# Attention with two gated layers on one core: all four full key tiles enter the values' product as float32, and three kinds of tiles span two PSUM banks

## The chip, the core and the metric

One core of a Trainium2 chip runs the whole program. Its engines run from queues of their own: TensorE (PE, with the weight loads shown as PEld), VectorE (DVE), ScalarE (ACT), GpSimd (POOL), and SyncE (SP), which issues all DMAs. The metric is the device time in microseconds, the median of three runs.

## What is computed

```python
# q, k, v: (4, 8, 576, 64) float32
q_rot, k_rot = rotate(q), rotate(k)                    # rotary embedding over d = 64
scores = matmul(q_rot, k_rot.T) / sqrt(64)
attn = exp(scores - max(scores)); attn /= attn.sum() + 1e-9
x = (attn @ v) -> (2304, 512)                          # heads side by side
x = (sigmoid(x @ w_gate) * (x @ w_val)) @ w_out        # d_ff 1536
h = x @ w_in2
out = where(h > 0, h, exp(min(h, 0)) - 1) @ w_out2     # d_ff 2048
```

The weights of the two layers come as float64, q, k and v as float32.

## The kernel before

**Two stages.** The first some 360 us are attention, 32 heads one after the other (in 16 pairs). The two layers follow; they are not touched by the change. In `first_chunk` and `split_all` (L611 to L622, L145) the weights of the first layer's first chunk are taken apart by VectorE, ScalarE and GpSimd while the last heads are still computed.

**Precision.** A product of two float32 matrices is mostly made of three products of `float32r` parts (a high part and the rest). For the scores the parts of q and k stand one above the other in the 128 rows of a buffer `W`, so that two products (`K1` by `Q1`, `K2` by `Q2`) give the sum, and a row of `W` holds the negative maxima, which so come off in the product itself. For the values there are two ways. A *split* tile (`KINDS` names the engine that makes its low part: key tiles 0 and 2 VectorE, tile 1 GpSimd) has its exponential written twice by ScalarE, once as float32 (`e`, L462) and once as float32r (`ph`, L464); `low_part` (L468) subtracts, and three products follow (L497 to L499) with a v that was split by `split_v` (L388). The *full* tile (`KINDS` None: tile 3) is written once and multiplied as float32 (L494). The last 64 keys (t = ST = 4, the tail) are one stack `pt` of high and low part and take two products (L491, L492). Heads 30 and 31 (`LF`) multiply all their tiles as float32 with `last_v` (L487).

**The order of work.** It is written out by hand: a *slot* for each head, of ten *steps* (NSTEP), two for each of the five key tiles. Slot i does the scores of head i, the maxima of head i + 2 and the values of head i - 1, interleaved step by step (L623 to L637); `at(slot, step, f)` puts anything else beside a step (with .5 ahead of the next step's scores, else behind its values). Every engine takes its instructions in the order in which they are written. A step of slot i is: two score products of one half (288 columns) of key tile t (L459), ScalarE's exponentials, one maxima product (L409) with VectorE's reduction (L412), and the values of one key tile for one half (L482 on). The scores and the transposes of q and k (`split`, L316) take one-bank tiles from `ps_qk` (3 buffers), the maxima from `ps_mt` (3), the values from `ps_pv` (2).

**Maxima.** `max_row` (L420) transposes a head's maxima, ScalarE copies the row, and a DMA puts it into `W`, where that head's scores need it. It is at step 1.5 of the slot ahead of the head, `max_all` (which joins the two halves' maxima) at step 2, so for all but head 0 the row holds the first half's maxima alone.

**SP's queue** carries, in the order of the text: loads of k and q (L599, step 0 of even slots), tails (L602), v (L603: three loads of 256-byte pieces for a group of four heads, at slot 4g - 1, step 6, and `load_vf` for the full tile), the moves of q's and k's parts into `W` (`move`, L344), the row of maxima (L426), and the four short transfers of the sums' reciprocals (`inverse`, L519).

**GpSimd** does the rotary embedding of all pairs but the first (`rope_ops`, L286), the low part of tile 1, v's low parts and the normalization (L545).

## Time and profile before

| | us |
|---|---|
| median of 3 runs | 1217.23 (1215.57 to 1217.28) |
| the profiled execution's own time | 1214.78 |
| its span, first to last instruction | 1213.0 |
| attention up to the first product of the layers | 364.73 |
| from there to the end | 848.27 |

| busy of the span | PE | PEld | DVE | ACT | POOL |
|---|---|---|---|---|---|
| us | 1163.2 | 983.2 | 995.6 | 499.4 | 689.2 |

The trace gives start and duration of every instruction, and for idle time the event that ended it. A matmul's record is longer than its share of TensorE: records overlap, and the pace is the distance from start to start in a stretch without waits. A float32 matmul is recorded as two (x2).

### The profile page before, as it was taken

The page shows a single profiled execution, that of the slowest core. Times are in us where ns is not written, and L with a number is a line of the kernel's source. Part 1 is how long each engine was busy: PE and PEld are TensorE (multiplying, and loading weights), DVE is VectorE, ACT ScalarE, POOL GpSimd, SP SyncE. Part 2 cuts the span into 40 slices and gives each one's busy share as a digit, 9 for nine tenths or more (in the row PEclk, how much of TensorE's full clock was granted, in tenths as well). Part 3 has the DMA queues.
Part 4 walks back from the last instruction along what each step waited for, and adds up shares of the span by engine and source line. Part 5 has one row for each costly group of instructions (what it writes and reads, how often), then busy time and mean ns, then how long its engine had stood idle before and what let it go on. Part 6 is the DMA issues. An engine that isn't in the chain of part 4 may idle for free.

```text
span 1213.0 us, 17583 instructions
## 1 busy us (share of the span) xinstructions
PE 1163.2 (96%) x5956; PEld 983.2 (81%) x5956; DVE 995.6 (82%) x2024; ACT 499.4 (41%) x1251; POOL 689.2 (57%) x731
## 2 busy tenths in 40 slices
PE   5898999999889999999999999999999999999998
PEld 4787888887857888888888888888888887888887
DVE  8888887887798987867777676778999999999844
ACT  3777777877744532122222222344422222222221
POOL 8977888887355555443444344666554545545421
PEclk9999999999999999999999999999999999999999
DMA  7676666755523121111111111101111111110004
GB/s 186 138 154 140 137 151 140 158 131 128 137 73 97 36 70 53 51 37 36 53 39 49 52 36 35 35 20 51 53 35 53 35 52 36 53 36 18 1 35 122
DMA packets 71146, 89.53 MB, mean 74 GB/s; under 512 B 35920, under 2 KB 44400, under 8 KB 71056
## 3 DMA queue, kind: packets, MB, share of 16 engines
q1 hardware_dynamic: 71056, 88.41, 28.4%
q8 instruction: 47, 0.77, 0.3%
q14 instruction: 43, 0.35, 0.1%
HBM read 56.01 MB, written 4.87 MB: 50 GB/s over the span
## 4 chain that ended last, share of the span: by engine, by line
PE 58%; DVE 9%; ACT 1%; issue 0%
PE h L680 12%; PE h L681 12%; PE h L682 12%; PE o L680 8%; PE o L681 8%; PE o L682 8%; DVE z L763 2%; DVE g L706 1%; DVE g L705 1%; DVE ca L130 1%; DVE cm L137 1%; DVE cm L127 1%; DVE ce L124 1%; DVE ce L133 1%; DVE cm L125 1%
## 5 line engine op out<-in xcount | busy, mean ns | idle before, releaser
L712 POOL TENSOR_TENSOR gl<-g,gh 128x512 fp32r<-128x512 f32 (+1 forms) x140 | 168.6, 1204 | 326.2 <-ACT gh L711 260.4
L711 ACT CAST gh<-g 128x512 fp32r<-128x512 f32 (+1 forms) x140 | 81.2, 580 | 306.6 <-DVE g L706 172.0
L459 PE MATMUL s<-W 128*128 128x288 f32 (+1 forms) x640 | 164.2, 339 | 22.9 <-DMA W<-row 9.6
L680 PE MATMUL h<-xh,wh 128*128 128x512 f32 (+1 forms) x480 | 177.3, 369 | 1.7 <-ACT xh L665 1.3
L681 PE MATMUL h<-xl,wh 128*128 128x512 f32 (+1 forms) x480 | 177.5, 370 | 1.0 <-DVE xl L666 1.0
L682 PE MATMUL h<-xh,wl 128*128 128x512 f32 (+1 forms) x480 | 177.1, 369 | 0.0
L138 POOL TENSOR_TENSOR ca<-ca,wh 128x256 f32<-128x256 f32 x136 | 113.8, 837 | 94.6 <-DVE cm L134 89.0
L412 DVE TENSOR_REDUCE MX<-mt 128x1 f32<-128x288 f32 (+1 forms) x320 | 132.6, 444 | 23.4 <-PE mt L409 22.0
L462 ACT ACTIVATE e<-s 128x288 f32<-128x288 f32 (+1 forms) x320 | 127.7, 411 | 50.1 <-PE s L459 10.8
L135 ACT CAST wh<-ca 128x256 fp32r<-128x256 f32 x136 | 55.3, 407 | 215.9 <-DVE ca L130 215.9
L459 PEld LDWEIGHTS s<-W 128*128 128x128 f32 (+1 forms) x640 | 101.1, 185 | 48.2 <-ACT ph L464 13.8
L140 POOL TENSOR_TENSOR wl<-ca,cm 128x256 fp32r<-128x256 f32 x136 | 113.0, 831 | 18.5 <-DVE cm L137 11.4
L681 PE MATMUL h<-yl,wh 128*128 128x512 f32 (+1 forms) x320 | 117.7, 368 | 0.0
L682 PE MATMUL h<-yh,wl 128*128 128x512 f32 (+1 forms) x320 | 117.7, 368 | 0.0
L680 PE MATMUL h<-yh,wh 128*128 128x512 f32 (+1 forms) x320 | 117.7, 368 | 0.0
L680 PE MATMUL o<-wh,gh 128*128 128x512 f32 x288 | 112.8, 392 | 1.6 <-DVE z L763 1.2
L681 PE MATMUL o<-wl,gh 128*128 128x512 f32 x288 | 112.2, 390 | 0.0
L682 PE MATMUL o<-wh,gl 128*128 128x512 f32 x288 | 112.1, 389 | 0.0
L701 DVE TENSOR_TENSOR g<-h,g 128x512 f32<-128x512 f32 (+1 forms) x60 | 38.2, 637 | 88.6 <-PE h L682 85.8
L409 PE MATMUL mt<-W 128*128 128x288 f32 (+1 forms) x320 | 100.5, 322 | 7.5 <-DVE MX L412 4.5
L680 PEld LDWEIGHTS h<-xh,wh 128*128 128x128 f32 x480 | 90.9, 189 | 17.9 <-ACT xh L665 1.7
L681 PEld LDWEIGHTS h<-xl,wh 128*128 128x128 f32 x480 | 90.8, 189 | 16.4 <-DVE xl L666 1.5
(116 smaller groups left out, 2875.2 us busy)
## 6 DMA issues: line engine op xcount, KB each, us to landing
W<-hl SPq DMA_DIRECT2D x89, 288.0 KB
raw<-in_moe_w_out_dram SPq DMA_DIRECT2D x28, 512.0 KB
raw<-in_moe_w_in_dram SPq DMA_DIRECT2D x16, 512.0 KB
raw<-in_moe_w_gate_dram SPq DMA_DIRECT2D x12, 512.0 KB
raw<-in_moe_w_val_dram SPq DMA_DIRECT2D x12, 512.0 KB
rb<-d SPq DMA_DIRECT2D x32, 144.0 KB
k<-in_k_dram SPq DMA_DIRECT2D x16, 256.0 KB
q<-in_q_dram SPq DMA_DIRECT2D x16, 256.0 KB
```

What stands on the lines that cost most here:

```text
L135: nc.scalar.copy(h, a)
L138: nc.gpsimd.tensor_tensor(out=a, in0=a, in1=h.bitcast(F32), op=ALU.subtract)
L140: nc.gpsimd.tensor_tensor(out=l, in0=a, in1=mf, op=ALU.add)
L409: nc.tensor.matmul(m[0:n, 0:HS], lhsT=operand(i, "Q1", t * P, n), rhs=operand(i, "K1", a * HS, HS), start=True, stop=True)
L412: nc.vector.tensor_reduce(out=MX[i % 3][0:n, a, t : t + 1], in_=m[0:n, 0:HS], axis=AX.X, op=ALU.max, negate=True)
L459: nc.tensor.matmul(s, lhsT=operand(i, st, t * P, n), rhs=operand(i, mv, a * HS, HS), start=st == "K1", stop=st == "K2")
L462: nc.scalar.activation(e[:, c], s, AF.Exp)
L680: nc.tensor.matmul(ps, lhsT=ah, rhs=bh, start=j == 0, stop=False)
L681: nc.tensor.matmul(ps, lhsT=ah, rhs=bl, start=False, stop=False)
L682: nc.tensor.matmul(ps, lhsT=al, rhs=bh, start=False, stop=j == n - 1)
L711: nc.scalar.copy(hi, g)
L712: nc.gpsimd.tensor_tensor(out=lo, in0=g, in1=hi.bitcast(F32), op=ALU.subtract)
```

## The change

All four full key tiles are handled as the full tile was, in all 32 heads; `KINDS`, `LF`, `last_v` and the split of v's full tiles go. Scores, maxima and the transposes of q or k use tiles of two banks, one half (288 columns) in each, and one exponential, one reduction (over both axes) or one copy handles both; so `max_all` goes. `ps_qk` has 2 such tiles, `ps_mt` 1. v of four heads comes in one load and GpSimd copies it into `VF`. The two half-wide products of the rotary embedding become one with the halves' order reversed in the read. Steps move: `max_row` from 1.5 to 0.5, k's and q's loads from step 0 to 3 (tails 4), v's load from slot 4g - 1 step 6 to slot 4g - 2 step 8, `split_v` from steps 1 and 5 to 5 and 7, a pair's transposes from four places (5.5 to 10.5) to two (5.5 and 9.5), the first move from step 11 to 12.

```diff
-    KINDS = ("vector","gpsimd","vector",None)
-        ps_qk = ...tile_pool(name="ps_qk", bufs=3, ...)
-        ps_mt = ...tile_pool(name="ps_mt", bufs=3, ...)
+        ps_qk = ...tile_pool(name="ps_qk", bufs=2, ...)
+        ps_mt = ...tile_pool(name="ps_mt", bufs=1, ...)
 def load_v(g):
-            t = raws["v", g] = v_p.tile([P, 4, NS, D], F32, tag="v", name=f"v{g}")
-            for n in range(NS):
-                nc.sync.dma_start(out=t[:, :, n], in_=tiles_of_v(b, h, 4, SP[n]))
+            load("v", 4 * g, 4, v_p)
             load_tails("vv", g, v_p)
-        def load_vf(pr): ...
 def rope_ops(pr, which, eng):
-            for a in range(2):
-                lo, hi = slice(a * hd, (a + 1) * hd), slice((1 - a) * hd, (2 - a) * hd)
-                tt(out=sv[..., lo], in0=x[..., hi], in1=sin[..., lo], op=ALU.mult)
-                yield
+            two = lambda y: y.rearrange(f"{axes} (two d) -> {axes} two d", two=2)
+            tt(out=two(sv), in0=two(x)[..., ::-1, :], in1=two(sin), op=ALU.mult)
+            yield
 def split(pr, which):          # one tile for all five transposes
+            T = ps_qk.tile([P, 1024], F32, tag="qk", name=f"T{which}{pr}")[:, 0:S]
...
             nc.scalar.copy(hi, T)
             nc.vector.tensor_tensor(out=lo, in0=T, in1=hi.bitcast(F32), op=ALU.subtract)
 def split_v(pr, piece):
             if piece == 0:
-                nc.scalar.copy(vs[..., D : 2 * D], x)
-                nc.gpsimd.tensor_tensor(out=vs[..., 0:D], in0=x, in1=vs[..., D : 2 * D].bitcast(F32), op=ALU.subtract)
+                nc.gpsimd.tensor_copy(VF[par][..., 0:D], x)
+        def both_halves(ps, n):
+            return ps.rearrange("p (a s) -> p a s", a=2)[0:n, :, 0:HS]
 def maxima(i, h):              # at odd steps, both halves
+            m = both_halves(ps_mt.tile([P, 1024], F32, tag="mt", name=f"mt{i}_{t}"), n)
+            for a in range(2):
+                nc.tensor.matmul(m[:, a], lhsT=operand(i, "Q1", t * P, n), rhs=operand(i, "K1", a * HS, HS), ...)
+            nc.vector.tensor_reduce(out=MX[i % 3][0:n, t : t + 1], in_=m, axis=AX.XY, op=ALU.max, negate=True)
-        def max_all(i): ...
 def max_row(i):
-            m = ps_mt.tile([P, 512], F32, tag="mt", name=f"mr{i}")
+            m = ps_qk.tile([P, 1024], F32, tag="qk", name=f"mr{i}")
 def scores(i, h):              # at even steps, both halves
+                e = probs[i, t] = e_p.tile([P, S], F32, tag="ef", name=f"e{i}_{t}", bufs=2 * ST)
+            s = both_halves(ps_qk.tile([P, 1024], F32, tag="qk", name=f"s{i}_{t}"), n)
+            for st, mv in (("K1", "Q1"), ("K2", "Q2")):
+                for a in range(2):
+                    nc.tensor.matmul(s[:, a], lhsT=operand(i, st, t * P, n), rhs=operand(i, mv, a * HS, HS), ...)
+            nc.scalar.activation(e.rearrange("p (a s) -> p a s", a=2), s, AF.Exp)
+            if t == ST:
+                nc.scalar.activation(probs[i, t][TL:P]..., s, AF.Exp)
+                at(i, h + 2.5, low_part, e, probs[i, t])
 def values(i, h):
+            if t == ST:  ...            # the two products of the tail, as before
+            else:
+                nc.tensor.matmul(out_ps, lhsT=VF[par][:, ab, t], rhs=e, start=t == 0, stop=False)
-            at(*((i - 2, 9) if i == 0 else (i - 1, 2)), max_all, i)
-            at(*((i - 2, 9) if i == 0 else (i - 1, 1.5)), max_row, i)
+            at(*((i - 2, 9) if i == 0 else (i - 1, 0.5)), max_row, i)
-                at(s0, (1, 5)[piece], split_v, pr, piece)
+                at(s0, (5, 7)[piece], split_v, pr, piece)
-            slot, step = {3: (-1, 9), 4: (1, 0)}.get(pr, (2 * pr - 8, 0))
+            slot, step = {3: (-1, 9), 4: (1, 3)}.get(pr, (2 * pr - 8, 3))
-            at(4 * g - 1, 6, load_v, g)
+            at(4 * g - 2, 8, load_v, g)
```

## Rows read from the trace of the kernel before

**Rows 1.** Busy time by stretch: window, length, busy us (count) each engine, PEclk, DMA.
```profile
33.28:326.64 293.36, 271.32 (x1734) 238.67 (x1735) 240.81 (x517) 225.63 (x672) 232.78 (x238) 0.97 0.64 143
326.64:364.73 38.09, 31.44 (x166) 24.38 (x164) 36.70 (x84) 21.15 (x62) 21.12 (x24) 0.96 0.26 70
364.73:1213.00 848.27, 840.80 (x3984) 705.95 (x3984) 690.26 (x1364) 240.08 (x488) 406.40 (x422) 1.00 0.15 46
120.40:123.60 3.20, 3.20 (x16) 3.06 (x15) 2.93 (x6) 1.86 (x6) 3.07 (x5) 0.50 0.58 123
349.10:356.30 7.20, 7.14 (x36) 5.20 (x34) 6.93 (x16) 3.90 (x12) 4.36 (x6) 1.00 0.28 75
```

**Rows 2.** TensorE in order of time, slot 29: start, us, line, out<-in, count.
```profile
326.64 0.42 PE L459 MATMUL s<-W 128*128 128x288 f32 x2
...
327.44 0.42 PE L459 MATMUL s<-W 128*128 128x288 f32 x2
...
329.40 0.29 PE L409 MATMUL mt<-W 128*128 128x288 f32 x1
329.53 0.65 PE L494 MATMUL pv<-e,VF 128*128 128x288 f32 x2
...
330.27 0.29 PE L409 MATMUL mt<-W 128*128 128x288 f32 x1
...
330.94 0.29 PE L409 MATMUL mt<-W 128*128 128x288 f32 x1
```

**Rows 3.** TensorE in order of time: slot 31, values in float32; a pair's transposes.
```profile
349.86 0.64 PE L459 MATMUL s<-W 128*128 128x288 f32 x2
350.34 0.65 PE L487 MATMUL pv<-e,last_v 128*128 128x288 f32 x2
350.61 0.64 PE L459 MATMUL s<-W 128*128 128x288 f32 x2
...
301.70 0.38 PE L330 MATMUL Tk<-ident,rk 128*128 128x128 f32 x2
...
302.22 0.47 PE L459 MATMUL s<-W 128*64 128x288 f32 x2
```

**Rows 4.** Waits from 33.28 to 326.64: who waited for whom, us, times, longest.
```profile
PE s L459 <- DMA W<-row: 9.6, 5, 2.2
PE s L459 <- ACT ph L464: 5.5, 5, 3.3
ACT VS L393 <- DMA v<-in_v_dram: 10.8, 7, 4.7
PEld s L459 <- ACT ph L464: 13.6, 29, 3.5
```

**Rows 5.** SP's issues in slot 12, then TensorE at the start of slot 13.
```profile
154.19 1.27 SPq L192 DMA_DIRECT2D k<-in_k_dram  x1
...
157.47 0.76 SPq L426 DMA_DIRECT2D W<-row  x1
...
160.09 0.40 PE L459 MATMUL s<-W 128*128 128x288 f32 x1 [1.83 <-DMA W<-row]
```

**Rows 6.** Groups by shape, 33.28 to 326.64: count, busy us, mean ns, idle before.
```profile
L412 DVE TENSOR_REDUCE MX<-mt 128x1 f32<-128x288 f32 x224 | 94.0, 444 | 20.3 <-PE mt L409 19.1
L464 ACT ACTIVATE ph<-s 128x288 fp32r<-128x288 f32 x168 | 68.2, 406 | 0.0
L471 DVE TENSOR_TENSOR pl<-e,ph 128x576 fp32r<-128x576 f32 x56 | 57.2, 1021 | 0.0
L471 POOL TENSOR_TENSOR pl<-e,ph 128x576 fp32r<-128x576 f32 x28 | 40.1, 1432 | 6.9 <-ACT ph L464 6.9
L471 DVE TENSOR_TENSOR pt<-e,pt 64x576 fp32r<-64x576 f32 x28 | 26.3, 938 | 0.6
```

**Rows 7.** Before the first head's scores: DVE's first maxima, TensorE's first scores.
```profile
14.51 3.85 DVE L412 TENSOR_REDUCE MX<-mt 128x1 f32<-128x288 f32 x10
...
24.96 1.17 PE L459 MATMUL s<-W 128*128 128x288 f32 x4
```

More of the change, by code (lines that the diff above doesn't have):

```diff
@@ L55, in attention_moe_moe_kernel @@
     NC2 = w_in2.shape[1] // FC
-    KINDS = ("vector","gpsimd","vector",None)
-    FP = [t for t, kind in enumerate(KINDS) if kind is None]
-    SP = [t for t, kind in enumerate(KINDS) if kind is not None]
-    NS, NF = len(SP), len(FP)
     assert D == 64 and TL == 64 and NK == NHP
@@ L247, in attention_moe_moe_kernel @@
         W = [[const.tile([P, 4 * S + TL], F32R, name=f"W{par}{ab}") for ab in range(2)] for par in range(NPAR)]
[L250 to L251 removed]
+        VF = [const.tile([P, 2, ST, 2 * D], F32, name=f"VF{par}") for par in range(2)]
         VT = [const.tile([P, 2, 3 * D], F32R, name=f"VT{par}") for par in range(2)]
[L253 removed]
+        MX = [small_p.tile([P, ST + 1], F32, name=f"MX{j}") for j in range(3)]
         def constants(par):
@@ L286, in rope_ops @@
         def rope_ops(pr, which, eng):
-            hd = D // 2
             if which == "t":
@@ L314, in attention_moe_moe_kernel, with split @@
         parts = {}
[L316 to L323 removed]
+        def split(pr, which):
+            if which == "k":
+                parts[pr] = hl_p.tile([P, 4, S], F32R, tag="hl", name=f"hl{pr}")
             r, rt = rot[pr, which], rot[pr, "t"]
             o = 0 if which == "q" else TL
[L326 to L340 removed]
+            T = ps_qk.tile([P, 1024], F32, tag="qk", name=f"T{which}{pr}")[:, 0:S]
+            for c in range(0, SM, P):
+                nc.tensor.transpose(T[:, c : c + P], r[:, c // P].rearrange("p h d -> p (h d)"), ident)
+            nc.tensor.transpose(
+                T[:, SM:S], rt[o : o + TL].rearrange("p h d -> p (h d)"), ident[o : o + TL, o : o + TL]
+            )
+            hi, lo = (parts[pr][:, n] for n in ((0, 1) if which == "k" else (2, 3)))
             nc.scalar.copy(hi, T)
@@ L348, in move @@
             slots = W[pr % NPAR][ab][:, 0 : 4 * S].bitcast(F32).rearrange("p (j s) -> p j s", j=4)
-            if pr == 1:
-                hk, lk, hq, lq = (x.bitcast(F32) for x in parts[pr])
-                nc.sync.dma_start(out=slots[z, 1], in_=lk[r])
-                nc.sync.dma_start(out=slots[r, 0:2], in_=hk[r].unsqueeze(1).to_broadcast([D, 2, S]))
-                nc.sync.dma_start(out=slots[z, 2], in_=hq[r])
-                nc.sync.dma_start(out=slots[r, 2], in_=hq[r])
-                nc.sync.dma_start(out=slots[r, 3], in_=lq[r])
-                return
             src = parts[pr].bitcast(F32)
@@ L455, in scores @@
-            e, hi, lo, _ = probs[i, t]
-            c = slice(a * HS, (a + 1) * HS)
-            s = ps_qk.tile([P, 512], F32, tag="qk", name=f"s{i}_{h}")[0:n, 0:HS]
-            for st, mv in (("K1", "Q1"), ("K2", "Q2")):
-                nc.tensor.matmul(
-                    s, lhsT=operand(i, st, t * P, n), rhs=operand(i, mv, a * HS, HS), start=st == "K1", stop=st == "K2"
-                )
-            nc.scalar.activation(e[:, c], s, AF.Exp)
-            if hi is not None:
-                nc.scalar.activation(hi[:, c], s, AF.Exp)
-                if a == 1:
-                    at(i, h + 1.5, low_part, i, t)
@@ L468, in low_part @@
-        def low_part(i, t):
-            e, hi, lo, _ = probs[i, t]
-            eng = nc.gpsimd if t < ST and KINDS[t] == "gpsimd" else nc.vector
-            eng.tensor_tensor(out=lo, in0=e, in1=hi.bitcast(F32), op=ALU.subtract)
+            if a == 1:
+                return
+            if t == ST:
+                e = e_p.tile([P, S], F32, tag="e", name=f"e{i}_{t}")[TL:P]
+                probs[i, t] = p_p.tile([P, S], F32R, tag="pt", name=f"pt{i}")
+            else:
+                e = probs[i, t] = e_p.tile([P, S], F32, tag="ef", name=f"e{i}_{t}", bufs=2 * ST)
@@ L473, in attention_moe_moe_kernel, with low_part @@
+        def low_part(e, pt):
+            nc.vector.tensor_tensor(out=pt[0:TL], in0=e, in1=pt[TL:P].bitcast(F32), op=ALU.subtract)
         us, sums, ps = {}, {}, {}
@@ L567, in attention_moe_moe_kernel @@
         for which in "kq":
-            for half in range(2):
-                at(-5, 1, split, 0, which, half)
+            at(-5, 1, split, 0, which)
             at(-5, 1, copies, 0, which)
         at(-5, 1, move, 0, 1)
-        for (which, half), st in zip((("k", 0), ("k", 1), ("q", 0), ("q", 1)), (10, 11, 13, 14)):
-            at(-2, st, split, 1, which, half)
+        for which, st in (("k", 11.5), ("q", 13.5)):
+            at(-2, st, split, 1, which)
         at(-1, 10, move, 1, 0)
```

126 lines of the change are left out of this document (24 added, 102 removed).

## The prediction

> **What bounds the kernel now.** I read the busy time by stretch first [rows 1]. From 364.73 on, the layers keep TensorE at 840.80 of 848.27 us; nothing of the change lies there. What it can move is the 365 us ahead: slots 1 to 28 (33.28 to 326.64, 293.4 us or 10.48 a slot), a start of 33.3 us and an end of 38.1 us. Second comes TensorE in order of time. In a stretch without waits a step with a split tile takes 0.80 us (326.64 to 327.44), one with the full tile 0.87 (329.40 to 330.27), a tail step 0.67 (330.27 to 330.94) [rows 2]. The tail step is five float32r products, so one is 0.134. A slot has six, two and two of these: 4.80 + 1.74 + 1.34 = 7.9 us. A pair's q and k add four groups of transposes; one with the tail's takes 0.52 [rows 3], two of the four lack it, so I put 0.4 each: 14 pairs x 4 x 0.4 = 22. Dense, slots 1 to 28 would be 28 x 7.9 + 22 = 243 us. They take 293, so TensorE loses 50 us to waiting although its records show it 271 us busy [rows 1]: records overlap and hide short waits.
>
> Third, the waits. Five heads' scores wait 9.6 us for the row of maxima [rows 4]. In slot 12 its DMA is issued at 157.47, behind k's load of 154.19 and what follows it, and TensorE starts again only at 160.09 [rows 5]. After such a wait the granted clock is 0.50, the 1.2 GHz level: 120.40 to 123.60 is one of five stretches in these slots [rows 1]. At half the clock 3.2 us do the work of 1.6, so they cost about 8 us. ScalarE waits 10.8 us for v's loads, and every exponential queued behind that copy waits too; TensorE's scores wait 5.5 us for ScalarE and its weight loads 13.6, in 29 pieces [rows 4]. The rest of the 50 us is of that short kind: a one-bank tile is released only after two exponentials, and these wait in turn for buffers that the subtractions hold.
>
> **The change, part by part.** *TensorE, slots 1 to 28.* Six split steps a slot become full ones: 0.87 - 0.80 = 0.07 each. From heads 30 and 31, whose values are all float32: a step of 0.75 us (349.86 to 350.61) less two scores at 0.134 is 0.48 for one product [rows 3], against three at 0.134 = 0.40, so 0.08. I take 0.077: 28 x 6 x 0.077 = 13 us more, all on the path. Dense becomes 256.
>
> The Trainium skill, "FP8 and Floating Point Precision" (TensorE Precision Notes), says that true FP32 takes four passes through the array, which speaks against the change. Four passes at the trace's 0.134 would be 0.54 and not 0.48; the trace nearly agrees, and by the rule the slots would lose some 10 us more.
>
> *ScalarE* loses six `ph` exponentials of 0.406 a slot [rows 6] and v's wide copy; wide exponentials save the fixed part of half their number. *VectorE* loses two subtractions of 1.021 a slot, *GpSimd* one of 1.432 [rows 6]; GpSimd gains a copy of v (512 elements a row, no row like it; between nothing and those 1.432, hidden either way, since its next user is five steps off). Ten reductions of 0.444 become five over 576 columns. Bounds for one: two at the pace of the first head's ten, 2 x 3.85/10 = 0.77 [rows 7], or two whole, 0.89 [rows 6]; I take 0.77. The reversed read in the rotary embedding lies between half and the whole of the two products that it replaces, on GpSimd, off the path. None of this lies on the path by itself; it removes what makes the scores wait. I do not price these waits one by one: what counts is what still waits afterwards.
>
> *SP.* The row comes at step 0.5, ahead of all loads (step 3 or 4) and of the first move; it then has some eight steps, over 7 us, where the late one needed about 2.5 (157.47 to 160.09 [rows 5]). The 9.6 us and the low clock behind them go. The load of v is one transfer 8 steps earlier, and its reader is four steps later. But at step 8 it waits in SP's queue for GpSimd's copy of step 5 and the tail's of step 7, and the next row is queued behind it: it would have to be held for over 4 us to be felt. Two buffers of scores instead of three, one of maxima: these are the added waits.
>
> *What waits afterwards.* (a) One buffer for maxima. From the start of the two products (0.27), about 0.16 until the reduction starts and its 0.77, the buffer is free after 1.2 us. TensorE comes back after six products at 0.134 and two at 0.48 = 1.76. So the reduction may be 0.56 late. Ahead of it, once a slot, VectorE has the tail's low part, 0.938 on the mean [rows 6]: about 0.4 lost. (b) Score tiles share two buffers with the transposes and the row's transpose. q's tile is released only after ScalarE's copy and VectorE's subtraction (each near 0.75, by size between the 0.406 for 288 columns and the 1.021 for 576 [rows 6], plus 0.15), 1.65 us; the row's transpose wants it after scores and values, 4 x 0.134 + 0.48 = 1.0. That is 0.6 once a pair, 0.3 a slot. Of the sum of 0.7 a slot I take 0.65, 18 us in all, since not every late start meets a full queue; ends 0.2 (both covered) and 1.5 (the slower rival). So slots 1 to 28: 256 + 18 = 274, or 19 us less.
>
> *The start.* The first two heads' maxima run before there is other work. Ten reductions took 3.85 us back to back [rows 7]; with one buffer five take 1.2 each, 6.0: 2 us later, and the second head's likewise overlap the transposes of pair 1. Slot 0 loses its low parts. I take +1.2 (bounds -1 to +3) until slot 1.
>
> *The end.* From 326.64 to 364.73 VectorE is busy 36.70 of 38.09 us [rows 1], with the weights' split. It loses head 29's two low parts and about 0.13 on each pair of reductions, and gains the tails' low parts of heads 30 and 31 (1.9). I take -1.5 (bounds -4 to +1).
>
> **The sum.** -19 + 1.2 - 1.5 = -19.3. The profiled run's own 1214.78 (span 1213.0) becomes 1195.5; against the median of 1217.23 it is 1198.
>
> With s us lost per slot the time is 1179.5 + 28 s; it meets 1217 at s = 1.33.
>
> **Rivals.**
> *All cover holds* (s = 0.2): with ScalarE, VectorE and GpSimd so much lighter TensorE runs dense. For: slots 29 and 31 hold the dense paces for several us on end [rows 2, 3]. Against: the single maxima buffer. 1185.
>
> *Half of the waits stay* (s = 1.1), for instance because VectorE's and ScalarE's wide pieces arrive in larger lumps: 1210.
>
> *The row stays late*: SP is held at v's load or a move, and the 9.6 us with the low clock of about 1.6 in four of those places come back: +16, 1214, no difference. Against it: the move ahead of the loads is by more than the 2.2 us that the longest such wait took [rows 4].
>
> *Slower: the single maxima buffer decides.* If the reduction starts on average 0.86 late and not 0.56, TensorE loses 0.3 at each of five tiles: s = 1.5, 1221. It decides from 0.83 late on (1.33 / 5 = 0.27 over the slack). For: VectorE's subtractions already take 1.021 on the mean [rows 6], and the copies of `u` and the wide subtraction of q and k lie between reductions. Against: VectorE's load falls from 8.6 us a slot (240.81 / 28 [rows 1]) by over two.
>
> *The float32 product at four full passes*: 0.06 more in each of six products a slot, 10 us: 1208. Against it is the 0.48 of heads 30 and 31 [rows 3]. (The Trainium skill's page named above has this rule.) That the clock falls under float32 products is not borne out either: 349.10 to 356.30 has it at 1.00 [rows 1].
>
> **How the numbers follow.** Forecast (1192 to 1205) 0.54; all cover 0.17; half stay 0.11; row late 0.06; slower 0.09; four full passes 0.03. The measurement can tell about 0.2%, 2.4 us. Faster: 0.54 + 0.17 + 0.11 + 0.03 and a part of the row's = 0.87; same 0.05; slower 0.08. For 8 in 10 the range reaches up to the half case and down to that of full cover: 1186 to 1211.
>
> **What would show it.** In the trace after: two records of a float32 product from start to start 0.48 us; no score waiting for the row in slots 2 to 28 and no stretch of clock 0.50 there; slots of 9.0 to 10.1 us; where TensorE waits, maxima for VectorE's reduction and the row's transpose for q's or k's subtraction; first scores near 26.5 and not 24.96 [rows 7]; the layers' stretch as long as now. I am wrong if maxima wait at most tiles, if the exponentials are late for float32 products, or if SP is found holding the row.

## The result, and the profile after

The kernel after takes 1224.35 us (median of 6 runs, 1219.87 to 1225.03) against 1216.4 (1215.4 to 1218.08): a ratio of 1.0059, 95% interval 1.0042 to 1.0076. It is slower, where 1198 was forecast. Its profiled execution took 1219.87 us, with a span of 1218.1, against 1214.78 and 1213.0. It was the shortest of its six executions (the others took 1224.07 to 1225.03), so of a loss of 8 us by the medians this trace shows 5.1. The stretches of [rows 1] in the trace of after (window, length, busy us and count of TensorE, weight loads, VectorE, ScalarE, GpSimd; granted clock, DMA share, GB/s):

```profile
41.23:325.34 284.11, 268.65 (x1565) 221.64 (x1564) 175.59 (x265) 153.59 (x293) 146.95 (x162) 1.00 0.65 146
325.34:361.40 36.06, 28.70 (x155) 22.53 (x153) 33.78 (x77) 19.07 (x40) 17.11 (x22) 1.00 0.24 70
361.40:1218.10 856.70, 851.26 (x3984) 706.78 (x3984) 690.16 (x1364) 241.03 (x488) 406.21 (x422) 1.00 0.15 45
```

| stretch | before | after | difference | forecast |
|---|---|---|---|---|
| until slot 1 | 33.28 | 41.23 | +7.95 | +1.2 |
| slots 1 to 28 | 293.36 | 284.11 | -9.25 | -19 |
| slot 29 to the layers | 38.09 | 36.06 | -2.03 | -1.5 |
| layers | 848.27 | 856.70 | +8.43 | 0 |

The four differences sum to the +5.1 between the spans. The engines beside TensorE did get lighter in the slots as forecast, VectorE from 240.81 to 175.59 us, ScalarE from 225.63 to 153.59, GpSimd from 232.78 to 146.95, and the granted clock is 1.00 there; yet half of the gain is missing, and two stretches lost some 8 us each.

**The start**, VectorE's maxima and TensorE's products in order of time, where [rows 7] had ten reductions back to back:

```profile
15.28 0.85 PE L360 MATMUL mt<-W 128*128 128x288 f32 x2 [1.20 <-DVE MX L363]
16.98 0.85 PE L360 MATMUL mt<-W 128*128 128x288 f32 x2 [0.85 <-DVE MX L363]
...
14.49 0.74 DVE L363 TENSOR_REDUCE MX<-mt 128x1 f32<-128x576 f32 x1
16.17 0.76 DVE L363 TENSOR_REDUCE MX<-mt 128x1 f32<-128x576 f32 x1 [0.94 <-PE mt L360]
...
30.50 1.17 PE L393 MATMUL s<-W 128*128 128x288 f32 x4
36.02 0.53 PE L360 MATMUL mt<-W 128*128 128x288 f32 x2 [0.25 <-DVE MX L363]
...
36.59 0.76 DVE L363 TENSOR_REDUCE MX<-mt 128x1 f32<-128x576 f32 x1 [0.62 <-PE mt L360]
37.97 0.76 DVE L363 TENSOR_REDUCE MX<-mt 128x1 f32<-128x576 f32 x1 [0.62 <-PE mt L360]
```

The two engines alternate: TensorE waits 0.85 for the reduction and VectorE 0.94 for the products. A tile takes 1.70 us (15.28 to 16.98), and still 1.38 (36.59 to 37.97) later on. The granted clock is on record from 35.2 on, at 1.00 (in the kernel before from 28.1); ahead of that the trace has no level. But the four scores of 30.50 start 0.24 us apart, and from 35.20 on scores start 0.13 to 0.14 apart, a ratio of 1.8, near that of the two levels, 1.2 and 2.4 GHz. In the kernel before the same step lies at 28.1. So the lower level is inferred here and not read, and it ends 7 us later than before. Two maxima products have a record of 0.85 under it and of 0.53 at 1.00 (36.02). The first scores come at 30.50 and not at 24.96.

**The slots**: waits from 41.23 to 325.34 (who waited for whom, us, times, longest), where [rows 4] had the row, `ph` and v's load:

```profile
PEld mr L367 <- ACT e L396: 14.7, 14, 1.1
PEld mt L360 <- DVE MX L363: 12.7, 19, 1.7
DVE r L453 <- DMA r<-d: 7.8, 11, 1.9
PE mr L367 <- ACT e L396: 5.9, 10, 0.6
PE mt L360 <- DVE MX L363: 5.1, 12, 1.2
```

No score waits for the row any more. What waits is the row's transpose, once in each odd slot, and the maxima. In slot 5 (TensorE, ScalarE, VectorE in order of time):

```profile
81.33 0.79 PE L393 MATMUL s<-W 128*128 128x288 f32 x4
81.95 0.65 PE L421 MATMUL pv<-e,VF 128*128 128x288 f32 x2
83.23 0.28 PE L367 MATMUL mr<-ident,MX 128*5 128x128 f32 x1 [0.62 <-ACT e L396]
...
90.76 0.43 PE L393 MATMUL s<-W 128*128 128x288 f32 x2
...
81.43 0.64 ACT L312 CAST hl<-Tq 128x576 fp32r<-128x576 f32 x1 [0.43 <-PE Tq L308]
82.10 0.40 ACT L437 ACTIVATE SUM<-pv 1x288 f32<-1x288 f32 x1
82.52 0.65 ACT L396 ACTIVATE e<-s 128x576 f32<-128x576 f32 x1
...
82.11 0.76 DVE L313 TENSOR_TENSOR hl<-Tq,hl 128x576 fp32r<-128x576 f32 x1 [0.83 <-ACT hl L312]
```

The row's transpose needs one of the two score buffers. One holds q's tile until VectorE's subtraction ends at 82.87, the other the slot's first scores until their exponential ends at 83.17; that one is queued behind q's copy and the copy of a sum (L437, 0.40). The transpose starts 0.06 after it; thirteen odd slots (3 to 27) have the same gap of 0.62. From its first scores to the next slot's (81.33 to 90.76) this slot takes 9.43.

The maxima, in slot 24 (VectorE, then TensorE):

```profile
274.67 0.21 DVE L453 RECIPROCAL r<-r 128x9 f32<-128x9 f32 x1 [1.05 <-DMA r<-d]
274.80 0.39 DVE L435 COPY u<-pv 64x288 f32<-64x288 f32 x1
275.21 1.33 DVE L402 TENSOR_TENSOR pt<-e,pt 64x576 fp32r<-64x576 f32 x1
276.47 0.74 DVE L363 TENSOR_REDUCE MX<-mt 128x1 f32<-128x576 f32 x1
...
277.27 0.53 PE L360 MATMUL mt<-W 128*128 128x288 f32 x2 [0.65 <-DVE MX L363]
```

Everything that stands ahead of a reduction on VectorE, here the tail's low part, delays the release of the one maxima buffer, and TensorE's next products wait. What more buffers are worth there is measured further down.

**The layers**: TensorE in order of time in an even chunk and in an odd one:

```profile
539.83 0.40 PE L595 MATMUL o<-gl,wh 128*128 128x512 f32 x1
...
541.01 0.39 PE L594 MATMUL o<-gh,wh 128*128 128x512 f32 x1
...
605.77 0.39 PE L596 MATMUL h<-xh,wl 128*128 128x512 f32 x1
...
607.13 0.39 PE L596 MATMUL h<-xh,wl 128*128 128x512 f32 x1
```

Five steps from 539.83 to 541.01 are 0.236 each, six from 605.77 to 607.13 are 0.227. TensorE waits for nothing in either, and the granted clock is 1.00 in both. In the kernel before the even chunks run at 0.227 too.

### The profile page after: what moved, and what is told of

It is laid out like the page before. It is cut to its first block, busy times and chain, and to the rows that moved or that the text cites. A ratio compares the mean times of both kernels' runs of the same rounds, so it can differ in the third digit from the quotient of the medians.

```text
span 1218.1 us, 16453 instructions
## 1 busy us (share of the span) xinstructions
PE 1169.8 (96%) x5776; PEld 965.8 (79%) x5776; DVE 923.5 (76%) x1740; ACT 423.8 (35%) x835; POOL 605.2 (50%) x652
## 3 DMA queue, kind: packets, MB, share of 16 engines
q1 hardware_dynamic: 56704, 88.11, 28.1%
## 4 chain that ended last, share of the span: by engine, by line
PE 83%; DMA 7%; DVE 6%; SPq 2%; ACT 1%; issue 1%; POOL 0%; DVEq 0%; POOLq 0%; ACTq 0%
PE h L595 14%; PE h L596 14%; PE h L594 14%; PE o L595 10%; PE o L594 10%; PE o L596 10%; PE pv L421 4%; DMA r<-d 4%; PE s L393 3%; PE mt L360 3%; DVE MX L363 2%; DVE pt L402 1%; DMA v<-in_v_dram 1%; DMA d<-r 1%; ACT hl L312 1%
## 5 line engine op out<-in xcount | busy, mean ns | idle before, releaser
L363 DVE TENSOR_REDUCE MX<-mt 128x1 f32<-128x576 f32 (+1 forms) x160 | 120.5, 753 | 91.1 <-PE mt L360 90.4
L421 PE MATMUL pv<-e,VF 128*128 128x288 f32 x512 | 164.0, 405 | 0.7 <-DVE u L435 0.7
L396 ACT ACTIVATE e<-s 128x576 f32<-128x576 f32 (+1 forms) x160 | 103.8, 649 | 124.2 <-PE s L393 105.5
L393 PE MATMUL s<-W 128*128 128x288 f32 (+1 forms) x640 | 138.1, 339 | 1.8 <-ACT e L396 1.8
L393 PEld LDWEIGHTS s<-W 128*128 128x128 f32 (+1 forms) x640 | 97.2, 181 | 17.9 <-ACT e L396 2.9
L360 PE MATMUL mt<-W 128*128 128x288 f32 (+1 forms) x320 | 91.3, 368 | 17.3 <-DVE MX L363 13.3
```

The source lines that it names most:

```text
L360: nc.tensor.matmul(m[:, a], lhsT=operand(i, "Q1", t * P, n), rhs=operand(i, "K1", a * HS, HS), start=True, stop=True)
L363: nc.vector.tensor_reduce(out=MX[i % 3][0:n, t : t + 1], in_=m, axis=AX.XY, op=ALU.max, negate=True)
L393: nc.tensor.matmul(s[:, a], lhsT=operand(i, st, t * P, n), rhs=operand(i, mv, a * HS, HS), start=st == "K1", stop=st == "K2")
L396: nc.scalar.activation(e.rearrange("p (a s) -> p a s", a=2), s, AF.Exp)
L421: nc.tensor.matmul(out_ps, lhsT=VF[par][:, ab, t], rhs=e, start=t == 0, stop=False)
```

## Experiments

**The whole change again**, on another chip.

> The changed kernel itself, on the same chip and beside the same runs of before as the next three. The changed kernel with the maxima's tiles widened was 13 us faster than the changed kernel's median, though the layers account for 8.4 to 9.1 only; the other four had been timed on another chip. Theory: the parts seen in the traces are all, and the changed kernel takes 1220 here, 4 us over before. Rival: it has something more that the traced execution did not show, and takes 1224 here too.

1221.94 us, ratio 1.0045 (1.0032 to 1.0058); slots 283.93, layers 856.42. The loss is the kernel's, not one chip's. The time lies between the 1220 of the theory and the 1224 of its rival. Slot 1 starts at 42.94 here, 1.7 later than in the first trace.

### The layers: where the tiles lie

Nothing in the layers' code differs, but the maxima's three tiles shrank from 40 to 20 bytes a partition. With the rounding and the padding that follow, all that is allocated behind them on the left side of SBUF moved down by 96 bytes. The weights of even chunks lie on the right side and stayed; those of odd chunks lie on the left and moved along.

```
-MX = [small_p.tile([P, ST + 1], F32, ...) for j in range(3)]
+MX = [small_p.tile([P, 2, ST + 1], F32, ...)[:, 0] for j in range(3)]
```

> The changed kernel with the three maxima tiles allocated at their former size (10 numbers a row, of which 5 are used), so that everything allocated behind them on the left side of the memory moves back by 96 bytes to where it stood before the change. Theory A (addresses): the layers' stretch, 848.3 us before and 856.7 after, lasts 848 again, and the whole is some 8.4 us shorter than the changed kernel: 1216. Theory B (the layers are slower for another reason, such as what the attention leaves behind or the order of the weights' split): the stretch stays at 856 to 857 and the time at 1224. In both the first scores stay at 30.5 us and slots 1 to 28 at 284.

Layers 847.53, slots 282.05; 1211.0 us, ratio 0.9954 (0.9941 to 0.9967). The layers' loss is gone with 20 unused bytes a tile. (Runs with tiles of this width are called "wide `MX`" below.) The reverse, on the kernel before:

```
-align(128 + 4 * 64, "pad_acc")
+align(128 + 4 * 64 + 96, "pad_acc")
```

> The kernel before with nothing but the padding behind the small tiles 96 bytes shorter: every tile allocated on the left stands where it stands after the change, the right side (the weights of even chunks) does not move. Theory A: the layers' stretch rises from 848.3 to some 856.7, in even chunks alone, the whole by 8 us to 1225. Theory B: nothing moves, 1216 to 1217.

Layers 856.78; 1227.18 us, ratio 1.0088 (1.0074 to 1.0102). And the right side moved as far as the left, on the changed kernel:

```
-align(32, "pad_r", side="right")
+align(32 - 96, "pad_r", side="right")
```

> The changed kernel with the right side shifted too, so that left and right start at the same place within 256 bytes again (160), though neither at a multiple of 256. If what counts is where the two operands of a product stand to each other, the layers' stretch is 848 again and the time 1216. If what counts is that each starts at a multiple of 256 (or 64) bytes, odd chunks, whose tiles are all on the left, would have been slow in the changed kernel too (they are not), and here all chunks would be alike: 848 or 865. Theory B: 857, 1224.

Layers 847.56; 1214.02 us, ratio 0.9977 (0.9969 to 0.9986). TensorE in 532 to 562 us (length, busy us and count of products, clock, DMA share, GB/s) with the wide maxima, with the kernel before shifted, and with both sides shifted:

```profile
532.00:562.00 30.00, 30.00 (x134) 1.00 0.17 53
```

```profile
532.00:562.00 30.00, 30.00 (x130) 1.00 0.16 53
```

```profile
532.00:562.00 30.00, 30.00 (x134) 1.00 0.12 36
```

134 products or 130 in the same 30 us, always busy. It is not the address of either operand that counts: with both moved the pace is the full one. It is the one relative to the other. Only an offset of 96 bytes was tried.

The slots of the last version take 286.48, against 284.11 in after, 283.93 in its repetition and 282.05 with wide `MX`. All four have the same instructions, so a difference of 2 us or so between the slots of two traces tells nothing by itself.

### The start: one maxima buffer

```
+            if i < 3 and t % 2 == 1:
+                tile_ = ps_qk.tile([P, 1024], F32, tag="qk", ...)
+            else:
                 tile_ = ps_mt.tile([P, 1024], F32, tag="mt", ...)
```

> The changed kernel, but the maxima of heads 0, 1 and 2 (computed ahead of or in slot 0) take every other tile from the scores' pool, which is nearly idle then: two buffers instead of one. Theory: each of the first heads' tiles costs a round of 1.70 us (products at the 1.2 GHz level 0.85, reduction 0.76), because TensorE and VectorE take turns; with two buffers the products run beside the reductions. First scores move from 30.5 to some 26.5 and slot 1 from 41.2 to some 35.5; the whole is 4 to 6 us shorter, 1219. Rival: the start is set by the transposes of pair 1 and the rotary embedding on GpSimd, and the first scores stay within 1 us of 30.5.

The first scores come at 26.6 and slot 1 at 36.13; 1215.17 us, ratio 0.9995 (0.9985 to 1.0005). TensorE's products and VectorE's reductions of the first head here:

```profile
13.39 1.30 PE L364 MATMUL mt<-W 128*128 128x288 f32 x4 [1.97 <-DVE W L335]
15.41 1.33 PE L364 MATMUL mt<-W 128*128 128x288 f32 x4 [0.72 <-DVE MX L367]
...
14.62 1.41 DVE L367 TENSOR_REDUCE MX<-mt 128x1 f32<-128x576 f32 x2
```

Two reductions now stand back to back, and of the 7.95 us until slot 1 5.1 come back. That the single maxima buffer costs the start is also seen in the runs further down: slot 1 comes at 37.35 and 38.09 with the maxima alone in one-bank tiles, and at 41.30 with the scores alone in them. Another 1.9 is there with the float32 values alone (slot 1 at 35.21, next run) and so is not the buffer's; in that trace the granted clock is 0.50 from 29.52 to 36.34, and the kernel before has no such stretch there. The last 0.9 stays without an account.

### Slots 1 to 28: values, and merged tiles

All four full tiles as float32 in the kernel before; one-bank tiles, three buffers each, and SP's order stay. v comes straight into `VF`, in four loads a pair, so that SP issues eight loads of v for four heads, where it issued five.

```
-    KINDS = ("vector","gpsimd","vector",None)
+    KINDS = (None,) * 4
-        p_p = ...tile_pool(name="p", bufs=2 * NS)
+        p_p = ...tile_pool(name="p", bufs=2)
-        LF = 30
+        LF = NHEAD
```

> The kernel before with one part of the change alone: all four full key tiles of all heads enter the values' product as float32 (one exponential, one product, no low part; v loaded straight into place in 256-byte pieces, four loads a pair, the tail's split kept), everything else, one-bank tiles, three buffers, the order of steps, the row's late place, as before. Theory A (the products cost TensorE 13 us more in slots 1 to 28, and the lighter ScalarE, VectorE and GpSimd give back more than that): slots 1 to 28 take 270 to 285 instead of 293, the whole 1200 to 1209. Rival B (TensorE was the bound of these slots and the waits are the row's and the clock's): slots 1 to 28 take 300 to 306, the whole 1223 to 1229.

1195.12 us, ratio 0.9821 (0.9808 to 0.9834). Its slots:

```profile
35.21:307.76 272.55, 265.19 (x1569) 224.51 (x1567) 196.57 (x462) 184.00 (x489) 149.27 (x191) 0.99 0.67 150
```

20.8 us less than before. So the values' part of the change is worth more than the whole of it was forecast at, and the rest of the change takes it back. Which merged tile does? First the maxima undone on the changed kernel, with wide `MX` (the minimum of the halves is as in the kernel before):

```
-ps_mt = ...tile_pool(name="ps_mt", bufs=1, ...)
+ps_mt = ...tile_pool(name="ps_mt", bufs=2, ...)
-            m = both_halves(ps_mt.tile([P, 1024], ...), n)
             for a in range(2):
+                m = ps_mt.tile([P, 512], ...)[0:n, 0:HS]
                 nc.tensor.matmul(...)
+                nc.vector.tensor_reduce(out=MX[i % 3][0:n, a, t : t + 1], in_=m, axis=AX.X, ...)
```

> The changed kernel with maxima alone in one-bank tiles again: two buffers of one bank instead of one of two, two reductions of 288 columns a tile, their minimum at step 0 of the next slot, the maxima's tiles as wide as before; scores and transposes stay in two-bank tiles. Theory that the single maxima buffer decides: it makes TensorE wait at the start (8 to 9 us until slot 1) and is most of what slots 1 to 28 lose against all values as float32 alone (282 against 272.6). Then slot 1 starts near 34 and slots 1 to 28 take 273 to 276: about 1194 to 1197. Rival: the two score buffers shared with the transposes decide in the slots; then slot 1 still starts near 34, since there only maxima run, but slots 1 to 28 stay at 280 to 283: about 1202. Second rival, VectorE: ten reductions of 0.44 instead of five of 0.75 are 0.65 us a slot more on the engine that is late, and the slots become longer than 283.

1213.33 us, ratio 0.9973 (0.9964 to 0.9982); slot 1 at 38.09, slots 287.24. I had put the minimum between the last reduction and the row's transpose, on the path. Without that:

```
-            at(*(... (i - 1, 0)), max_all, i)
+            at(*(... (i - 1, 2)), max_all, i)
```

> As the run with maxima in one-bank tiles, two buffers, but the minimum of the halves stands at step 2, behind the row as in the kernel before, and no longer between the last reduction and the row's transpose. (From head 1 on the row is then the maximum over the first 288 key columns, as in the kernel before; the shift cancels in the quotient.) Theory that the single maxima buffer costs little once there is other work: slots 1 to 28 stay within 2 us of 282, what the changed kernel with wide maxima tiles takes, and the 5 us by which the run with the minimum was longer (287) were that minimum. Rival, the maxima buffer decides: with the minimum out of the way slots 1 to 28 fall to 275 or below. Either way slot 1 starts near 38, where the other run had it.

1207.29 us, ratio 0.9923 (0.9907 to 0.9939); slots 284.43, 2.8 less without the minimum. Two one-bank buffers for the maxima gain nothing in the slots as long as scores are merged; VectorE pays for them with ten reductions in place of five. Now the other half:

```
-ps_qk = ...tile_pool(name="ps_qk", bufs=2, ...)
+ps_qk = ...tile_pool(name="ps_qk", bufs=4, ...)
-            s = both_halves(ps_qk.tile([P, 1024], ...), n)
+            s = ps_qk.tile([P, 512], ...)[0:n, 0:HS]
+            c = slice(a * HS, (a + 1) * HS)
...
+            for c0, c1 in ((0, 256), (256, S)):
+                T = ps_qk.tile([P, 512], ...)[:, 0 : c1 - c0]
```

> The other half of the pair: scores, transposes and the row's transpose in one-bank tiles, four buffers of one bank instead of two of two, with two exponentials a tile and two copies and subtractions a transposed matrix; the maxima stay in one two-bank tile, allocated as wide as before. Single maxima buffer, theory: nothing in the start changes (slot 1 near 42) and slots 1 to 28 stay near 280: 1208 to 1211. Rival, the shared score buffers: q's tile is released a half at a time, the wait of the next row's transpose (5.9 us for its tile and 14.7 for its weight load in the changed kernel) mostly goes, and slots 1 to 28 take about 274: 1202. Worse than both: ScalarE's five more exponentials a slot (0.41 each against half of 0.65, so 0.4 us a slot) make scores late, slots above 283.

1198.25 us, ratio 0.9852 (0.9833 to 0.9871); slots 273.86. The row's transpose now waits like this, against 14.7 and 5.9 in after:

```profile
PEld mr L369 <- ACT SUM L441: 4.8, 14, 0.3
```

Both undone, three buffers of one bank each:

```
-ps_qk = ...bufs=2    -ps_mt = ...bufs=1
+ps_qk = ...bufs=3    +ps_mt = ...bufs=3
```

> The changed kernel with all its PSUM tiles back in one bank, three buffers of scores and transposes and three of maxima as in the kernel before, the row's transpose among the maxima again, the minimum at step 2; the float32 values, the one load of v, its copies, SP's order and the reversed read in the rotary embedding stay. Theory (merging costs, the rest of the change is right): start as before, slot 1 at 33 to 36; slots 1 to 28 at 270 to 274, as with the values alone (272.6) or scores alone undone (273.9); layers 847.5; 1190 to 1196 in all. Rival: SP's new order costs, which the two buffers hid: slots 1 to 28 above 280 as when the row and the loads alone were moved (301.6 against 293.4), 1203 or more.

1187.81 us, ratio 0.9766 (0.9752 to 0.978), the fastest of all runs. Its slots, its waits of TensorE for VectorE, and the start of slots 5 and 6:

```profile
35.43:300.71 265.28, 263.72 (x1565) 223.93 (x1564) 199.55 (x460) 179.91 (x489) 155.05 (x166) 1.00 0.69 157
```

```profile
PEld mt L362 <- DVE MX L365: 3.1, 13, 0.5
```

```profile
74.07 0.53 PE L399 MATMUL s<-W 128*128 128x288 f32 x2
...
82.64 0.43 PE L399 MATMUL s<-W 128*128 128x288 f32 x2
```

An odd slot (74.07 to 82.64) takes 8.57 us, without a wait; an even one has a pair's transposes and takes 10.03 at the least. Merging therefore costs 284.1 - 265.3 = 18.8 us here, or 16.8 against the merged version with wide `MX` (282.05), which this one has too: 8.6 with the maxima alone merged (273.86), 19.1 with the scores alone (284.43). They don't add up. The slots by kind, in us:

| | odd, 1 to 27 | even, 2 to 26 | slot 28 |
|---|---|---|---|
| after | 133.8 | 139.9 | 10.4 |
| after with wide `MX` | 135.5 | 136.5 | 10.1 |
| maxima alone undone | 133.8 | 140.7 | 10.0 |
| scores alone undone | 130.4 | 134.9 | 8.6 |
| both undone | 122.4 | 134.5 | 8.5 |

In the odd slots the maxima's buffer costs 8.0 (130.4 - 122.4), but only once the scores' tiles no longer cost more. The even slots and slot 28 gain from the scores' tiles alone (3.6 to 7.3 us in all, by the two merged traces), although it is the maxima that the trace shows waiting there: the name of a wait is not its cause. One thing more is undone with the maxima: the row holds the first half's maxima alone, as in the kernel before. What a row of both halves would cost in this version was not tried.

Two attempts to cure the merged version, both with wide `MX` (slots 282.05 without them). q's transposes a step earlier:

```
-("q", 11.5 if pr == 2 else 9.5)
+("q", 11.5 if pr == 2 else 8.5)
```

> The changed kernel with the maxima's tiles widened (1211.0) and the transposes of q one step earlier (8.5 instead of 9.5). Theory: in each of 14 odd slots the transpose of the row waits 0.6 us for the tile that q's transposes hold until VectorE's subtraction; a step earlier they are through in time, so 14 x 0.6 = 8 us less: 1203, odd slots of 8.9 instead of 9.45. Rival: the wait moves to the last key tile's scores or to the next head's first, which take the next tile of the two: 1209 to 1212.

1212.66 us, ratio 0.9971 (0.9959 to 0.9983); slots 282.30. The wait only changed its name:

```profile
PEld mr L367 <- DVE MX L363: 14.0, 13, 1.1
```

And the reciprocal three steps later:

```
-enumerate((0, 4, 8, 12) if late else (1, 5, 9, 13))
+enumerate((0, 4, 8, 12) if late else (1, 5, 12, 16))
```

> The changed kernel with its maxima tiles allocated as wide as before, and with steps 12 and 16 instead of 9 and 13 for the reciprocal of the sums and for the loads of its result. VectorE's queue, theory: in slots 8, 16, 20, 24 and 26 (11.0 to 11.6 us long) the reciprocal waits about 1 us for its DMA, and u, the tail's low part and a reduction are queued behind it while TensorE needs that reduction's buffer; three steps more let the DMA land first. The 1 us is felt in some five slots, so slots 1 to 28 shrink from 282 to about 277, the kernel by 4 to 5 us against that with wide tiles (1211), to about 1206. Rival: the reciprocal's wait only covers another lateness (GpSimd's products or q's tile), and the long slots stay within 1 us of what they were: 1210 to 1212.

1209.64 us, ratio 0.9939 (0.9925 to 0.9954); slots 281.46. VectorE's waits for that DMA, 6.0 us with wide `MX`, left the list, and the slots lost 0.6, which is no difference between two traces. What I had read in slot 24 as the cause of the long slots is no cause: the maxima were late without it.

### SP's order

The order alone, on the kernel before:

```
-            at(*(... (i - 1, 1.5)), max_row, i)
+            at(*(... (i - 1, 0.5)), max_row, i)
-            slot, step = {3: (-1, 9), 4: (1, 0)}.get(pr, (2 * pr - 8, 0))
+            slot, step = {3: (-1, 9), 4: (1, 3)}.get(pr, (2 * pr - 8, 3))
```

(and the tails' loads from step 0 to 4.)

> The kernel before with one part of the change alone: the row of maxima at step 0.5 and the loads of k, q and their tails at steps 3 and 4. Theory: the five waits for the row (9.6 us) go, and with them the low clock behind them (about 1.6 in each of four places): 10 to 16 us less, 1200 to 1206, slots 1 to 28 at 278 to 283. Rival: the loads now hold up something else in SP's queue (v's loads, which are as late as before, the reciprocals), or the heads that had waited are then as slow as their neighbours for other reasons, and under 5 us remain.

1221.52 us, ratio 1.0043 (1.0031 to 1.0056). The row's waits of [rows 4] are gone, and the slots are 301.63, 8.3 longer. Waits in them:

```profile
DVE r L532 <- DMA r<-d: 19.9, 13, 2.5
PEld s L459 <- ACT ph L464: 19.2, 40, 4.1
ACT e L462 <- POOL pl L471: 18.0, 6, 4.4
PEld mt L409 <- DVE MX L412: 15.1, 25, 1.4
```

TensorE waits for ScalarE, that for GpSimd, and VectorE for the reciprocal's DMA. I took this for the backlog of the splitting that the row's waits had hidden; then the same order should pay with float32 values alone.

> The kernel before with all four full tiles as float32 and nothing else merged (measured at 1195.1), and now with the row at step 0.5, the minimum of the maxima at step 0, and the loads at step 3 or 4. Theory: in the kernel before the row's waits hid a backlog on GpSimd, ScalarE and VectorE, so the earlier row alone gained nothing (1221.5); with the splitting of values and probabilities gone there is no backlog left, so the row waits go and with them the low clock behind them, 6 to 12 us: slots 1 to 28 at 262 to 267 instead of 272.6, 1184 to 1190. Rival: the reciprocal's and the tails' waits on VectorE take their place as they did without the float32 values: slots 271 to 275, 1194 to 1198.

1253.16 us, ratio 1.0309 (1.0282 to 1.0336): slots 329.22. Here too the minimum stood ahead of the row's transpose, behind a reciprocal that waited (from 40 to 320 us):

```profile
DVE r L523 <- DMA r<-d: 33.9, 11, 4.6
PEld mr L413 <- DVE MX L409: 30.7, 24, 3.8
```

With the minimum back at step 2, first the row alone moved, then the row and the loads:

> The kernel before with all full tiles as float32 (1195.1) and the row at step 0.5 instead of 1.5; the minimum stays at step 2 and the loads at step 0. Theory: the loads at step 0 are issued ahead of the row either way, and the row's 6.2 us of waits shrink only by the step's 0.9 us in six places or so: slots 1 to 28 at 266 to 271, 1189 to 1194. Rival: the earlier row asks for the last reduction before VectorE has it, and the wait moves to the row's transpose: 272 to 276, no gain. If this is as long as the run with the minimum ahead of the row (slots 329), the row's place did that and not the minimum.

> The same with the loads at step 3 or 4 as well: it differs from the run of 1253.2 only in the place of the minimum (step 2 instead of 0). Theory: that run was longer by 58 us because VectorE's reciprocal, which waits for its DMA (33.9 us in 11 pieces), stood ahead of the minimum, and the row's transpose, and with it TensorE, behind it; without the minimum in that chain slots 1 to 28 return to 265 to 276, 1188 to 1198. Rival: the loads at step 3 or 4 hold SP ahead of the reciprocal's DMA, whatever VectorE does: slots above 300.

1224.26 us, ratio 1.0071 (1.0053 to 1.0089), slots 304.95; and 1219.45, ratio 1.0035 (1.0021 to 1.005), slots 295.59. The minimum explains 34 of that run's 57 us, and the backlog theory fell: 23 us are lost with no splitting at all. Waits in the second:

```profile
DVE r L523 <- DMA r<-d: 47.8, 13, 5.4
PEld mt L400 <- issue: 27.5, 14, 2.9
PE mt L400 <- DMA W<-hl: 24.7, 14, 2.7
```

Moves and the reciprocal's DMAs come late from SP. In that version four loads of v a pair (1.91 us of SP in one place) stand between the row and the move. Taking them out:

```
+            load("v", 4 * g, 4, v_p)
-                at(s0 - 1, 1, load_vf, pr)
-                pass
+                nc.gpsimd.tensor_copy(VF[par][..., 0:D], x)
-                at(s0, (1, 5)[piece], split_v, pr, piece)
+                at(s0, (5, 7)[piece], split_v, pr, piece)
-            at(4 * g - 1, 6, load_v, g)
+            at(4 * g - 2, 8, load_v, g)
```

> The kernel before with all full tiles as float32, the row at step 0.5 and the loads at step 3 or 4 (1219.5), now with v in one load for two pairs and GpSimd's copy of its tiles instead of four loads a pair on SP at step 1. Theory: in that run the four issues (1.91 us in one place) stand between the row and the move, so the move, the reciprocal's DMA and the next maxima (waits of 23.3 and 25.9 us for the move) all come late; without them slots 1 to 28 fall from 295.6 to 265 to 272. Rival: the early row itself, held on SP until ScalarE has copied it (44 us), delays what is behind it: slots stay above 285.

1192.96 us, ratio 0.9809 (0.9792 to 0.9826); slots 267.09, 28.5 less:

```profile
DVE r L524 <- DMA r<-d: 15.3, 13, 2.8
PE mt L401 <- DMA W<-hl: 2.5, 3, 1.7
```

With four loads of v a pair the early row and loads cost 23 us against the float32 values alone (272.55); with one load for two pairs the slots are 5.5 shorter than those. This edit changes the number, the size and the time of v's transfers and the steps of `split_v` together, so which of them does it is not shown. Last, the order undone in the version without merged tiles:

> The changed kernel with all PSUM tiles in one bank (1187.8) and, on top, SP's order undone: the row at step 1.5 and the loads at step 0, as in the kernel before. What is left of the change is then the float32 values, v in one load with GpSimd's copy, and the reversed read. Theory: the order is what keeps the row from being late (0.5 us of such waits with it, 6.2 and the low clock behind them in the kernel before with the float32 values alone), so slots 1 to 28 become 271 to 274 instead of 265.3, 1194 to 1197. Rival: v's single load was the gain, since it takes eight issues a pair from SP, and the row finds SP free in either place: 265 to 267, 1187 to 1190.

1191.42 us, ratio 0.9784 (0.9769 to 0.9799); slots 267.76. With v in one load the order is worth 2.5 us in the slots, hardly more than two traces differ by, and the two ratios' intervals overlap. The larger part, 4.8 against the float32 values alone (272.55), is there without it: v's load, the moved transposes and the reversed read together.

## Why the prediction was wrong, point by point

**Layers: "nothing of the change lies there".** Wrong, +8.4 us. It was a reading of instructions, and no instruction changed; the addresses did. Without it the profiled run would have been 3 us shorter than before and not 5 longer; with 20 unused bytes a tile the ratio is 0.9954.

**Start: +1.2, bounds up to +3.** Wrong, +7.95. The mechanism (products and reduction alternate on one buffer) was the forecast's for the 5.1 us that a second buffer gives back; its price was not. The 1.9 that the float32 values alone bring was not in the sum at all. I took 1.2 us a tile: products from 0.27, a start of 0.16, 0.77 of reduction, all at the pace of slot 29. But ahead of 35.2 the products run slower, by their pace at the lower level (records of 0.85 against 0.53), which the first scores of [rows 7], 1.17 for four, already showed against [rows 2]. 1.70 us was measured there. At the recorded 1.00 it is 1.38: from the first product's start to the reduction's 0.57 (36.02 to 36.59), where I had 0.43, then 0.76 and 0.05 back.

**Values, ScalarE, VectorE, GpSimd.** Right: the float32 values alone take 20.8 us from the slots, more than the 19 forecast there for the whole change. A float32 product takes 0.48 from start to start (in slot 4 of after, 71.18 to 71.66). The Trainium skill, "FP8 and Floating Point Precision" (TensorE Precision Notes), has four passes for true FP32. The prediction took four whole products of 0.134, 0.54, for that, and this was misread: float32r products start 0.227 apart with 512 columns (605.77 to 607.13) and 0.117 with 256 (in the kernel before shifted, 605.82 to 607.11), so about 0.01 of a product does not grow with its columns. At 0.43 ns a column four passes over 288 are 0.49, an estimate, and with 0.48 the trace agrees with the Trainium skill there. The reduction takes 0.754 (forecast 0.77).

```profile
L363 DVE TENSOR_REDUCE MX<-mt 128x1 f32<-128x576 f32 x112 | 84.5, 754 | 49.6 <-PE mt L360 48.9
L396 ACT ACTIVATE e<-s 128x576 f32<-128x576 f32 x112 | 72.9, 651 | 82.6 <-PE s L393 76.9 <-PE pv L419 2.8 <-ACT SUM L437 0.3
```

**Slots: dense 256.** Too low by 4. Without a wait an odd slot takes 8.57 and an even one with its transposes 10.03 in the version without merged tiles: 14 x 18.60 = 260.4 (in fact some 259.6, since slot 28 has no transposes and slot 1 only q's). The slot was put at 7.9 + 6 x 0.077 = 8.4, without the row's transpose.

**Slots: added waits, 18 (0.65 a slot).** Both places were named, and 284.1 - 260.4 = 23.7 were lost, or 0.85 a slot. But the version with nothing merged still loses 4.9 of it (265.3 - 260.4), waits that the sum had at nothing. What merging adds, 16.8 to 18.8, is close to the 18, and that is luck. (a), put at 0.4 a slot, is 0.31 where it stands alone (8.6) and nothing beside (b); (b), put at 0.3, is 0.68 (19.1); and the two were added. In (b), q's tile against the row's transpose, odd slots without another wait take 9.43 against 8.57, so 0.86 a pair, 12 us, where 0.6 was put. What I left out is that ScalarE serves q's copy, the copy of a sum and the first exponential one after the other. What merging adds in the even slots and slot 28 goes with the scores' tiles too and not with (a), by the table above; by which chain was not shown. Of the rivals, "half of the waits stay" (s = 1.1) and "the single maxima buffer decides" (s = 1.5) lie beyond it. The latter is refuted as what decides: with two one-bank maxima buffers the slots stay at 284.4. Its time of 1221 is near the measured one by chance, since it has 298 us in the slots (256 + 28 x 1.5).

The step behind this was larger than the error in s. I asked what the merged tiles add to a slot that is freed from its waits, and set it against the whole gain; I did not price the same change without them. That one has slots of 265.3, and the 18 us that I booked as a side cost are about all that separates the change from it there (16.8 to 18.8).

**SP.** Right as a result for this change: no row waits, clock 1.00 in the slots. Wrong as a term of its own ("the 9.6 us and the low clock behind them go"): the same order on the kernel before lengthens the slots by 8.3. What carries it is v's single load with GpSimd's copy (28.5 us on top of the same order), which I had priced as harmless and not as the gain.

**End.** Right in its number, -2.03 against -1.5, and in part by luck. The float32 values alone leave the stretch at 38.00 and the version with one-bank tiles at 37.82, so head 29's low parts give almost nothing; it is the merged tiles that shorten it.

**The sum.** Slots missed by 9.8, the start by 6.8, the layers by 8.4, the end by -0.5: 24.4 us, and 1195.5 became 1219.9.

**What stays open.** Why the reciprocal's DMA and the moves come so much later when the row is early and SP full was read from waits, not isolated. Which of the two score buffers the row's transpose takes was not settled. Of the layers' offset, other sizes than 96 bytes were not tried. The reversed read of the rotary embedding and the new places of the transposes were never run by themselves.

## What to carry to other kernels

Fewer, larger PSUM tiles in the same banks mean fewer buffers: price each by the whole chain from the first product to the last reader's end, at the clock of the stretch where it runs, and try the rest of the change without them. Before a load, a row or a move is put ahead on a queue, count the issues that it then stands in front of; taking issues away (one load for four) can be worth more than any order. A tile that changes its size moves every tile behind it: compare the addresses of the largest products' operands before and after, and keep their distance.

## What the runs showed of the hardware that was not expected

A float32r product of 128x512 starts every 227 ns or every 234 ns with nothing waiting and the clock at 1.00, by the place of its two operands in SBUF relative to one another: moving one by 96 bytes costs the 7 ns, moving both gives them back. Over the layers of this kernel that is 8.4 to 9.2 us of 848.

Two engines that hand one buffer to and fro take 1.70 us a tile at the start of the program and 1.38 later on, where their own records are 0.85 + 0.76 and 0.53 + 0.76: 0.1 us of each round lies in no record, in either.
